# A searched issue order in which the two halves of 235 epilogue pairs stand as entries of their own

## The chip, the cores and the metric

The kernel runs on one core of a Trainium2 chip. The metric is the device time of one execution in microseconds (us). Its engines work side by side, each on its own list of instructions, in the order of that list: TensorE (PE; its weight loads are PEld), VectorE (DVE), ScalarE (ACT), GpSimd (POOL), and SyncE (SP), which only issues DMAs here. An instruction that needs another engine's result waits on a semaphore, and whatever stands behind it on its engine waits with it.

## The reference

The first part is an attention in which a query sees only the keys of its own cluster (4 batches, 8 heads, 768 positions, head size 64, 16 clusters); the second is a dense layer, a rational function and another dense layer over the 3072 tokens that come out.

```python
q_assign = np.argmax(einsum('bhsd,hcd->bhsc', q_n, c_n), axis=-1)   # k_assign likewise
mask = q_assign[:, :, :, None] == k_assign[:, :, None, :]
scores = np.where(mask, scale * (q @ k.transpose(0, 1, 3, 2)), -1e9)
attn = exp(scores - scores.max(-1)); attn = attn / (attn.sum(-1) + 1e-9)
x = (attn @ v).transpose(0, 2, 1, 3).reshape(3072, 512)
h = x @ w_in                                                        # 512 -> 2048
P = a[0] + a[1] * h + a[2] * h**2 + a[3] * h**3
Q = 1.0 + abs(b[0]) * abs(h) + abs(b[1]) * h**2
out = (P / (Q + 1e-6)) @ w_out                                      # 2048 -> 512
```

## The kernel before

The work is staged by batch (4), in a batch by pairs of heads (4) and by blocks of 256 queries (3). For each pair of heads, q and k are loaded, scaled and split into two fp16 halves, the clusters are found (`ptl` on PE at L1058, then on DVE `mx` L1072, `df` L1073, `df` L1076, `mxi` L1081, `oh` L1082), and the one-hot rows are written beside the operands (`tk` L1100) and turned by DMA. Batch 0 takes another path than the rest: scores with the keys on the partitions (`z` L1330), then `px` at L1349, sums at L1355, a reciprocal that is spread over the partitions on PE (`px` L1383), and the scaled result on DVE (`rw` L1392). Batches 1 to 3 compute `s` (L1162, a PSUM tile for 128 queries of one head), take the maximum on DVE (L1191), the exponential on ACT, the reciprocal of the sum (`su` L1210), and split the weights into `ah` (a high part on ACT, the rest on DVE at L1222, which is the last reader of the PSUM tile of `s`); a DMA turns them and PE multiplies them with v (`px` L1242). `vm`, `vt` and `vb` (L779 to L786) are the maximum of |v| of a batch.

The dense part of a block runs between these. It has 8 chunks of the 2048 columns, each in halves of 128 x 512 elements. `ph` (L1450) is x @ w_in in PSUM; 96 such halves are in the program. Each `ph` is read four times: by ACT (`u`, absolute value, and `t`, scale and offset) and by DVE (`t` at L1467 and `t` at L1468). POOL then computes the quadratic of Q (`s` at L1515, `s` at L1516; in a share of the halves ACT does the first), ACT a logarithm and an exponential of it, POOL the Newton factor (L1538), POOL or DVE the last step of P and its product with 1/Q (`t` at L1544 and L1545, or L1551), DVE the corrected quotient (L1556), then it is split into two fp16 halves (ACT L1560, POOL L1564) for the second matmul `po` (L1575). ACT instructions are all shown with L395, the line of a helper.

No instruction is issued while the program is written out: each becomes an entry of a list (`Plan.op`), numbered as it arises, and `Plan.emit` runs the entries in the order of the list `ORDER`, 4184 numbers that a search outside the program found. This one order decides the order on every engine, of the DMAs on SP, and which buffer of a ring a tile gets. An entry can hold several instructions; these then stand one behind the other on their engine, whatever the order says. Three such entries matter here:

```python
def poly(t=t, h=h, ph=ph, col=col):
    stt(out=t[h].ap, in0=ph.ap, scalar=col("rho")(), in1=t[h].ap, op0=ALU.mult, op1=ALU.mult)
    stt(out=t[h].ap, in0=t[h].ap, scalar=col("a1")(), in1=ph.ap, op0=ALU.add, op1=ALU.mult)
```

`poly` is on DVE (L1467 and L1468, 96 times), `square` on POOL (L1515 and L1516, 96 times), `times` on POOL (L1544 and L1545, 43 times).

Of the kernel before, what the change touches and what calls it, by code (L numbers as in the profile page):

```python
# [15 lines left out]
ALU = mybir.AluOpType  # L16
# [230 lines left out]
def clustered_attention_moe_kernel(  # L247
# [12 lines left out]
    nc = tc.nc  # L260
# [1149 lines left out]
    def moe(b, tb, vt):  # L1410
# [7 lines left out]
        for ci in range(NWC):  # L1418
# [5 lines left out]
            def col(name, ci=ci):  # L1424
                return lambda: gk.ap[:, COLS.index(name), ci : ci + 1]
# [240 lines left out]
```

## Time and profile before

| | before |
|---|---|
| runs, us | 930.46, 930.63, 931.91 (median 930.63) |
| the profiled execution's span, us | 930.4 |
| busy: PE | 863.5 us (93%) |
| busy: DVE, ACT, POOL | 835.6 (90%), 811.2 (87%), 729.3 us (78%) |
| chain that ended last | PE 54%, DVE 19%, ACT 9%, POOL 6%, issue 6%, DMA 5% |

The span of the profiled execution is 0.2 us under the median of the runs. Busy time is the time in which an engine has an instruction under way, summed over the whole span. The chain that ended last is followed back from the last instruction, at each step to what released it. No engine is idle for long, so what counts is in which stage an engine waits, and for whom; the page's 40 slices show PE below 90% in the first five of them, about 116 us.

### The profile page before, as it was taken

The page shows a single profiled execution, that of the slowest core. Times are in us where ns is not written, and L with a number is a line of the kernel's source. Part 1 is how long each engine was busy: PE and PEld are TensorE (multiplying, and loading weights), DVE is VectorE, ACT ScalarE, POOL GpSimd, SP SyncE. Part 2 cuts the span into 40 slices and gives each one's busy share as a digit, 9 for nine tenths or more (in the row PEclk, how much of TensorE's full clock was granted, in tenths as well). Part 3 has the DMA queues.
Part 4 walks back from the last instruction along what each step waited for, and adds up shares of the span by engine and source line. Part 5 has one row for each costly group of instructions (what it writes and reads, how often), then busy time and mean ns, then how long its engine had stood idle before and what let it go on. Part 6 is the DMA issues. An engine that isn't in the chain of part 4 may idle for free.

```text
span 930.4 us, 20764 instructions
## 1 busy us (share of the span) xinstructions
PE 863.5 (93%) x7705; PEld 581.1 (62%) x7705; DVE 835.6 (90%) x1503; ACT 811.2 (87%) x1558; POOL 729.3 (78%) x771
## 2 busy tenths in 40 slices
PE   1679998988899999999989999999999999999997
PEld 1357665656566666666666766666666675777663
DVE  6789999769989999999999999999999998899986
ACT  5577697989999999999999999999999998886774
POOL 2546789988999999999989988988989996464342
PEclk9989999989999999999999999999999999999999
DMA  7995765796977899998799879896987587501000
GB/s 200 232 249 130 190 193 148 177 230 138 188 133 154 164 161 203 155 167 163 155 162 180 164 135 169 178 188 110 208 150 150 92 165 130 121 2 33 8 24 23
DMA packets 360853, 137.70 MB, mean 148 GB/s; under 512 B 335665, under 2 KB 352049, under 8 KB 360753
## 3 DMA queue, kind: packets, MB, share of 16 engines
q1 hardware_dynamic: 360752, 136.39, 72.0%
q8 instruction: 60, 0.98, 0.4%
q14 instruction: 41, 0.33, 0.1%
HBM read 41.98 MB, written 6.29 MB: 52 GB/s over the span
## 4 chain that ended last, share of the span: by engine, by line
PE 54%; DVE 19%; ACT 9%; POOL 6%; issue 6%; DMA 5%; SPq 1%; ACTq 0%; DVEq 0%; POOLq 0%
PE ph L1450 18%; PE po L1575 18%; PE s L1162 7%; PE px L1242 5%; DVE ah L1222 3%; DVE s L1191 3%; DMA rvm<-in_v_dram 2%; PE s L1286 2%; DVE t L1467 1%; DVE t L1556 1%; ACT s L395 1%; PE px L1349 1%; DVE t L1468 1%; DVE top L1295 1%; PE z L1330 1%
## 5 line engine op out<-in xcount | busy, mean ns | idle before, releaser
L1450 PE MATMUL ph<-x,win 128*128 128x256 f16 x2304 | 273.1, 273 | 6.3 <-DVE t L1468 4.7
L1450 PEld LDWEIGHTS <-win 128*128 128x128 f16 x2304 | 223.2, 98 | 55.3 <-DVE t L1468 8.6
L1575 PE MATMUL po<-wout,s 128*128 128x512 f16 x1008 | 239.3, 379 | 0.7 <-POOL s L1564 0.7
L1191 DVE TENSOR_SCALAR_CACHE_REDUCE s<-s,cc 128x768 f32<-128x768 f32 x144 | 145.9, 1017 | 15.4 <-PE s L1162 14.8
L1575 PEld LDWEIGHTS <-s 128*128 128x128 f16 x1008 | 96.4, 98 | 101.2 <-issue 2.2
L1222 DVE SCALAR_TENSOR_TENSOR ah<-s,su,ah 128x768 f16<-128x768 f32 x144 | 144.9, 1011 | 5.6 <-ACT ah L395 5.3
L395 ACT ACTIVATE ah<-s,su 128x768 f16<-128x768 f32 x144 | 129.0, 901 | 7.8 <-DVE su L1210 7.2
L395 ACT ACTIVATE s<-s,nm 128x768 f32<-128x768 f32 x144 | 126.1, 876 | 7.3 <-DVE s L1191 4.9
L1162 PE MATMUL s<-sk,sq 128*128 128x384 f16 x576 | 117.8, 329 | 8.9 <-DVE ah L1222 7.9
L1516 POOL TENSOR_TENSOR s<-s,u 128x512 f32<-128x512 f32 x84 | 114.4, 1362 | 7.0
L1538 POOL TENSOR_TENSOR s<-s,u 128x512 f32<-128x512 f32 x72 | 99.1, 1378 | 7.0 <-ACT u L395 6.7
L1515 POOL TENSOR_SCALAR s<-u,g 128x512 f32<-128x512 f32 x84 | 69.6, 829 | 36.4 <-ACT u L395 33.6
L1564 POOL TENSOR_TENSOR s<-t,s 128x512 f16<-128x512 f32 x72 | 88.1, 1226 | 8.8 <-ACT s L1560 6.8
L1162 PEld LDWEIGHTS <-sq 128*128 128x128 f16 x576 | 52.2, 98 | 53.7 <-DVE ah L1222 17.9
L1556 DVE SCALAR_TENSOR_TENSOR t<-s,t 128x512 f32<-128x512 f32 x84 | 81.8, 973 | 0.8 <-POOL s L1538 0.5
L1242 PE MATMUL px<-at,vhi 128*64 128x256 f16 x864 | 75.2, 276 | 0.0
L395 ACT ACTIVATE u<-ph,gk 128x512 f32<-128x512 f32 x84 | 57.8, 688 | 9.3 <-PE ph L1450 8.7
L1468 DVE SCALAR_TENSOR_TENSOR t<-t,gk,ph 128x512 f32<-128x512 f32 x84 | 62.8, 748 | 3.0
L395 ACT ACTIVATE t<-ph,gk 128x512 f32<-128x512 f32 x84 | 65.4, 780 | 0.0
L1467 DVE SCALAR_TENSOR_TENSOR t<-ph,gk,t 128x512 f32<-128x512 f32 x84 | 62.1, 739 | 1.1 <-ACT t L395 1.0
L1545 POOL TENSOR_TENSOR t<-t,u 128x512 f32<-128x512 f32 x43 | 57.6, 1340 | 3.6
L1242 PE MATMUL px<-at,vlo 128*64 128x256 f16 x432 | 59.7, 273 | 0.0
(232 smaller groups left out, 1751.3 us busy)
## 6 DMA issues: line engine op xcount, KB each, us to landing
rwi<-in_moe_w_in_dram SPq DMA_DIRECT2D x16, 512.0 KB, 4.1
rwo<-in_moe_w_out_dram SPq DMA_DIRECT2D x16, 512.0 KB, 4.4
rk<-in_k_dram SPq DMA_DIRECT2D x32, 192.0 KB, 3.4
rq<-in_q_dram SPq DMA_DIRECT2D x32, 192.0 KB, 3.7
rvm<-in_v_dram SPq DMA_DIRECT2D x16, 384.0 KB, 3.8
rv<-in_v_dram SPq DMA_DIRECT2D x16, 384.0 KB, 4.1
out_dram<-ob SPq DMA_DIRECT2D x24, 256.0 KB, 2.9
sk<-sk SPq DMA_DIRECT2D x12, 192.0 KB, 3.4
```

What stands on the lines that cost most here:

```text
L395: lambda: nc.scalar.activation(out=out(), in_=in_(), func=func, **{a: (x() if callable(x) else x) for a, x in kw.items()}),
L1162: nc.tensor.matmul(sc.ap[:, i, :SH], lhsT=st["q" + x].ap[:, j, t, :], rhs=st["k" + x].ap[:, j, ks, :].rearrange("p t c -> p (t c)"), start ...
L1191: lambda nm=nm, view=view: ts(out=view(), in0=view(), scalar1=cc.ap[:, 0:1], scalar2=None, op0=ALU.mult, op1=ALU.min, accum_out=nm.ap),
L1222: lambda part=part, view=view, su=su: stt(out=part(1), in0=view(), scalar=su.ap, in1=part(0), op0=ALU.mult, op1=ALU.subtract),
L1242: nc.tensor.matmul(px.ap[j * D : (j + 1) * D, :], lhsT=vv.ap[:, j, kt, :], rhs=at[j].ap[:, p_, kt].rearrange("p t c -> p (t c)"), start=(i ...
L1450: nc.tensor.matmul(ph.ap[:, fi * TW : (fi + 1) * TW], lhsT=win[:, wpart, c, f * P : (f + 1) * P], rhs=xs[c].ap[:, xpart], start=(i == 0), ...
L1468: stt(out=t[h].ap, in0=t[h].ap, scalar=col("a1")(), in1=ph.ap, op0=ALU.add, op1=ALU.mult)
L1516: nc.gpsimd.tensor_tensor(out=sv(), in0=sv(), in1=uv(), op=ALU.mult)
L1538: lambda uv=uv, sv=sv: nc.gpsimd.tensor_tensor(out=sv(), in0=sv(), in1=uv(), op=ALU.mult),
L1556: lambda tv=tv, sv=sv: stt(out=tv(), in0=sv(), scalar=2.0, in1=tv(), op0=ALU.subtract, op1=ALU.mult),
L1564: lambda tv=tv, g16=g16, e=(nc.vector if kshare("gld", b, i_) else nc.gpsimd): e.tensor_tensor(out=g16(1), in0=tv(), in1=g16(0), op=ALU.su ...
L1575: nc.tensor.matmul(po[ti].ap, lhsT=g16(gg)[:, c0 : c0 + P], rhs=wout[:, wpart, f, :], start=(i == 0 and f == 0), stop=(i == 2 and f == NF ...
```

## The change

`ORDER` is replaced by another list, and the two instructions of each `poly`, `square` and `times` become two entries, so that the list has 4419 numbers. The operations, their operands, the tiles and the numbers of instructions on each engine stay as they are. The first half of `times` no longer names `u` as something it reads.

```diff
 ORDER = [int(i) for i in """
-3 376 377 28 375 374 4 5 6 40 7 8 0 9 379 381 382 10 29 383 32 30 388 31 391 380 33 34 392 44 384 41 490 42
...
-                def poly(t=t, h=h, ph=ph, col=col):
-                    stt(out=t[h].ap, in0=ph.ap, scalar=col("rho")(), in1=t[h].ap, op0=ALU.mult, op1=ALU.mult)
-                    stt(out=t[h].ap, in0=t[h].ap, scalar=col("a1")(), in1=ph.ap, op0=ALU.add, op1=ALU.mult)
-                dve(1523, poly, [ph, gk], [t[h]], u_ + h + kb("phr", b), [t_t], n=2)
+                dve(
+                    739,
+                    lambda t=t, h=h, ph=ph, col=col: stt(
+                        out=t[h].ap, in0=ph.ap, scalar=col("rho")(), in1=t[h].ap, op0=ALU.mult, op1=ALU.mult
+                    ),
+                    [ph, gk], [t[h]], u_ + h + kb("phr", b), [t_t],
+                )
+                dve(
+                    748,
+                    lambda t=t, h=h, ph=ph, col=col: stt(
+                        out=t[h].ap, in0=t[h].ap, scalar=col("a1")(), in1=ph.ap, op0=ALU.add, op1=ALU.mult
+                    ),
+                    [ph, gk], [t[h]], u_ + h + kb("phr", b), [t_t],
+                )
...
-                    def square(uv=uv, sv=sv):
-                        nc.gpsimd.tensor_scalar(out=sv(), in0=uv(), scalar1=g1c(BT), scalar2=1.0, op0=ALU.add, op1=ALU.mult)
-                        nc.gpsimd.tensor_tensor(out=sv(), in0=sv(), in1=uv(), op=ALU.mult)
-                    op("POOL", (2330, 3930)[k], square, [*us, g1], ss, uu + kb("sq", b), [s_t, u_t])
...
+                        [gk], tss, uu + kb("mul", b) - 0.2, [t_t],
```

`square` and `times` are parted in the same way. In the new order 43 of the 96 `poly` pairs have other DVE instructions between their halves (1 to 8), 38 of the 96 `square` pairs and 35 of the 43 `times` pairs other POOL instructions. Before, ACT's two reads of every `ph` stand ahead of DVE's two. Now that is so for 67 of them (for 17 more, ACT reads in the other order, t first), and in 12 ACT's absolute value comes behind a DVE read of the same tile: behind the first in 5, behind both in 7. The engines read one PSUM tile in turn, so each such place is a wait of one engine on another: 28 such waits of ACT on DVE and 13 of DVE on ACT, where there were 9 and none. On PE, 558 of 813 groups of matmuls stand at another place, by 1.8 places in the mean and 36 at most. Lines of the changed kernel are 11 higher up to `ph` (L1450 is L1461) and 34 higher from L1551 on (L1551 is L1585).

The first place is on DVE in the first 30 us, where the clusters of the first pair of heads are found (`mx0_0`, `df0_0`, `mxi0_0`, `oh0_0`, `tk20_0`) between the splitting of weights (`wwo`, L544 and L551). Before:

```order
L1010 SCALAR_TENSOR_TENSOR tk10_1_217<-rk0_1_178,ksc0_1_234,tk10_1_217 128x12x64
L544 TENSOR_SCALAR wwo0_0_304<-mwo0_0_300 128x512
L1072 TENSOR_REDUCE mx0_0_323<-ptl0_0_247 128x24
L551 SCALAR_TENSOR_TENSOR wwo0_0_304<-rwo0_0_226,wwo0_0_304 128x512
L1073 TENSOR_TENSOR df0_0_329<-ptl0_0_247,mx0_0_323 128x384
L1076 TENSOR_TENSOR df0_0_329<-df0_0_329,w16_74 128x384
L1081 TENSOR_REDUCE mxi0_0_340<-df0_0_329 128x24
L1082 TENSOR_TENSOR oh0_0_344<-df0_0_329,mxi0_0_340 128x384
L1100 TENSOR_SCALAR tk20_0_185<-oh0_0_344 128x12x48
```

The same stretch of DVE in the changed kernel:

```order
L1021 SCALAR_TENSOR_TENSOR tk10_1_218<-rk0_1_180,ksc0_1_227,tk10_1_218 128x12x64
L1083 TENSOR_REDUCE mx0_0_299<-ptl0_0_250 128x24
L1084 TENSOR_TENSOR df0_0_301<-ptl0_0_250,mx0_0_299 128x384
L555 TENSOR_SCALAR wwo0_0_305<-mwo0_0_303 128x512
L1087 TENSOR_TENSOR df0_0_301<-df0_0_301,w16_74 128x384
L562 SCALAR_TENSOR_TENSOR wwo0_0_305<-rwo0_0_231,wwo0_0_305 128x512
L1092 TENSOR_REDUCE mxi0_0_316<-df0_0_301 128x24
L1093 TENSOR_TENSOR oh0_0_318<-df0_0_301,mxi0_0_316 128x384
L1111 TENSOR_SCALAR tk20_0_205<-oh0_0_318 128x12x48
```

`mx` and the first `df`, the two readers of `ptl`, moved ahead of the first split of `wwo`, which waits for ACT's `mwo`.

The second place is on PE at the end of batch 0, where the maximum of |v| of batch 1 is turned (`vt1`) and the scores of its first block begin (`s1_0_0_1`, `s1_0_0_0`). Before:

```order
L1330 MATMUL z0_3_2_1_0_2682<-sq20_3_1769,sk20_3_1779 128x256
L1383 MATMUL px0_3_1_2594<-rw0_3_1_2669,pick_90 128x128 x2
L781 MATMUL vt1_2711<-ident_65,vm11_2705 1x128
L1162 LDWEIGHTS sq11_0_2202
L1162 MATMUL s1_0_0_1_2714<-sk11_0_2196,sq11_0_2202 128x384
L1162 LDWEIGHTS sq21_0_2565
L1162 MATMUL s1_0_0_1_2714<-sk21_0_2560,sq21_0_2565 128x384
```

The changed kernel on PE there, beginning with the third and fourth matmul of `s1_0_0_1` (the two ahead of them read alike, and ahead of those stand the last ones of `z0_3_2_1_1`):

```order
L1173 LDWEIGHTS sq11_0_2329
L1173 MATMUL s1_0_0_1_2683<-sk11_0_2277,sq11_0_2329 128x384
L1173 LDWEIGHTS sq21_0_2563
L1173 MATMUL s1_0_0_1_2683<-sk21_0_2561,sq21_0_2563 128x384
L792 MATMUL vt1_2688<-ident_65,vm11_2650 1x128
L1173 LDWEIGHTS sq11_0_2329
L1173 MATMUL s1_0_0_0_2690<-sk11_0_2277,sq11_0_2329 128x384
```

The four matmuls of `s1_0_0_1` moved ahead of `vt1`, and the spreading of `px0_3_1` (L1383) behind both score tiles.

The third place is on DVE in the middle of batch 2, ahead of its first `ah` of the second pair of heads; `mx2_2` and `df2_2` belong to the clusters of the third pair. Before:

```order
L1551 SCALAR_TENSOR_TENSOR t1_1_0_0_6622<-t1_1_0_0_6622,gk1_2792,u1_1_0_0_6594 128x512
L1210 RECIPROCAL su2_1_0_1_6878<-su2_1_0_1_6878 128x1
L1072 TENSOR_REDUCE mx2_2_6897<-ptl2_2_6829 128x24
L1222 SCALAR_TENSOR_TENSOR ah2_1_0_0_6887<-s2_1_0_0_6755,su2_1_0_0_6784,ah2_1_0_0_6887 128x768
L1222 SCALAR_TENSOR_TENSOR ah2_1_0_1_6899<-s2_1_0_1_6803,su2_1_0_1_6878,ah2_1_0_1_6899 128x768
L1073 TENSOR_TENSOR df2_2_6914<-ptl2_2_6829,mx2_2_6897 128x384
L1191 TENSOR_SCALAR s2_1_1_0_6906,nm2_1_1_0_6923<-s2_1_1_0_6906,cc2_1_5640 128x2x384
```

The same stretch of the changed kernel, also on DVE:

```order
L1233 SCALAR_TENSOR_TENSOR ah2_1_0_0_6789<-s2_1_0_0_6742,su2_1_0_0_6773,ah2_1_0_0_6789 128x768
L1083 TENSOR_REDUCE mx2_2_6872<-ptl2_2_6823 128x24
L1233 SCALAR_TENSOR_TENSOR ah2_1_0_1_6876<-s2_1_0_1_6765,su2_1_0_1_6780,ah2_1_0_1_6876 128x768
L1084 TENSOR_TENSOR df2_2_6879<-ptl2_2_6823,mx2_2_6872 128x384
L1479 SCALAR_TENSOR_TENSOR t1_1_1_0_6884<-ph1_1_1_0_6792,gk1_3490,t1_1_1_0_6884 128x512
L1202 TENSOR_SCALAR s2_1_1_0_6912,nm2_1_1_0_6917<-s2_1_1_0_6912,cc2_1_5506 128x2x384
L1486 SCALAR_TENSOR_TENSOR t1_1_1_0_6884<-t1_1_1_0_6884,gk1_3490,ph1_1_1_0_6792 128x512
```

`mx2_2` moved behind `ah2_1_0_0`, and a maximum of `s` (L1202) now stands between the halves of a `poly`. On PE, 12 matmuls of `po` instead of 6 stand between `ptl2_2` and `s2_1_1_0`.

## Rows read from the trace of the kernel before

**Rows 1.** The page: busy time of each engine.

```profile
PE 863.5 (93%) x7705; PEld 581.1 (62%) x7705; DVE 835.6 (90%) x1503; ACT 811.2 (87%) x1558; POOL 729.3 (78%) x771
```

**Rows 2.** Busy time of each engine by stretch of the span.

```profile
core 0: us, PE busy (x) PEld busy (x) DVE busy (x) ACT busy (x) POOL busy (x), PEclk, DMA share, GB/s
0.00:100.00 100.00, 66.36 (x670) 45.07 (x671) 78.30 (x178) 64.26 (x114) 52.67 (x73) 0.97 0.82 202
100.00:200.00 100.00, 89.69 (x1087) 63.62 (x1088) 85.50 (x159) 81.98 (x157) 86.14 (x104) 0.97 0.72 184
200.00:300.00 100.00, 93.23 (x844) 63.94 (x841) 88.12 (x163) 96.25 (x196) 90.76 (x97) 0.99 0.75 158
300.00:775.00 475.00, 464.10 (x4033) 310.00 (x4031) 449.35 (x818) 456.89 (x903) 431.94 (x445) 1.00 0.87 161
775.00:925.00 150.00, 149.05 (x1074) 98.20 (x1071) 134.31 (x189) 110.59 (x191) 67.76 (x56) 1.00 0.20 42
```

**Rows 3.** Waits, 300 to 775 us: total, times, longest (us).

```profile
PE s L1162 <- DVE ah L1222: 6.7, 12, 2.1
...
PE ph L1450 <- DVE t L1468: 2.3, 5, 0.7
```

**Rows 4.** Timeline of PE and DVE, first 30 us: start, duration, wait.

```profile
22.70 0.79 PE L1058 MATMUL ptl<-cen,sk 128*128 128x16 f16 x24
...
25.53 0.43 DVE L544 TENSOR_SCALAR wwo<-mwo 128x512 int32<-128x512 int32 x1 [1.85 <-ACT mwo L395]
25.88 0.55 DVE L1072 TENSOR_REDUCE mx<-ptl 128x24 f32<-128x384 f32 x1
26.34 0.68 DVE L551 SCALAR_TENSOR_TENSOR wwo<-rwo,wwo 128x512 int32<-128x512 int32 x1
...
27.53 0.36 DVE L1076 TENSOR_TENSOR df<-df,w 128x384 bf16<-128x384 bf16 x1
27.92 0.55 DVE L1081 TENSOR_REDUCE mxi<-df 128x24 bf16<-128x384 bf16 x1
28.51 0.56 DVE L1082 TENSOR_TENSOR oh<-df,mxi 128x384 f16<-128x384 bf16 x1
29.10 0.31 DVE L1100 TENSOR_SCALAR tk<-oh 128x576 f16<-128x576 f16 x1
```

**Rows 5.** Timeline of PE around 194 us.

```profile
193.90 0.27 PE L781 MATMUL vt<-ident,vm 128*1 128x128 f32 x1 [1.48 <-DVE rw L1392]
194.01 2.58 PE L1162 MATMUL s<-sk,sq 128*128 128x384 f16 x8
...
197.46 4.57 PE L1349 MATMUL px<-at,rv 128*64 128x256 f32 x24 [0.35 <-ACT vp_ln L395]
```

**Rows 6.** The same 24 matmuls of an earlier block, timeline of PE.

```profile
166.94 2.81 PE L1349 MATMUL px<-at,rv 128*64 128x256 f32 x24
```

**Rows 7.** Busy time by engine, 194 to 201 us; columns as in Rows 2.

```profile
194.00:201.00 7.00, 6.65 (x29) 3.41 (x29) 4.43 (x11) 5.91 (x14) 6.54 (x10) 0.52 1.03 258
```

**Rows 8.** Timeline of PE and DVE around 475 us.

```profile
472.00 1.46 PE L1575 MATMUL po<-wout,s 128*128 128x512 f16 x6
475.60 1.75 PE L1162 MATMUL s<-sk,sq 128*128 128x384 f16 x8 [2.14 <-DVE ah L1222]
477.19 1.03 PE L1575 MATMUL po<-wout,s 128*128 128x512 f16 x4
...
474.09 0.53 DVE L1072 TENSOR_REDUCE mx<-ptl 128x24 f32<-128x384 f32 x1
474.54 1.93 DVE L1222 SCALAR_TENSOR_TENSOR ah<-s,su,ah 128x768 f16<-128x768 f32 x2
```

**Rows 9.** Groups by line: busy us, mean ns, idle time before them.

```profile
L1468 DVE SCALAR_TENSOR_TENSOR t<-t,gk,ph 128x512 f32<-128x512 f32 x84 | 62.8, 748 | 3.0
...
L1556 DVE SCALAR_TENSOR_TENSOR t<-s,t 128x512 f32<-128x512 f32 x84 | 81.8, 973 | 0.8 <-POOL s L1538 0.5
```

**Rows 10.** A single instruction of L1556, timeline of DVE.

```profile
306.41 0.68 DVE L1556 SCALAR_TENSOR_TENSOR t<-s,t 128x512 f32<-128x512 f32 x1
```

More of the change, by code (lines that the diff above doesn't have):

```diff
@@ L1512, in moe @@
                 else:
-                    def square(uv=uv, sv=sv):
-                        nc.gpsimd.tensor_scalar(out=sv(), in0=uv(), scalar1=g1c(BT), scalar2=1.0, op0=ALU.add, op1=ALU.mult)
-                        nc.gpsimd.tensor_tensor(out=sv(), in0=sv(), in1=uv(), op=ALU.mult)
-                    op("POOL", (2330, 3930)[k], square, [*us, g1], ss, uu + kb("sq", b), [s_t, u_t])
+                    op(
+                        "POOL", 829,
+                        lambda uv=uv, sv=sv: nc.gpsimd.tensor_scalar(
+                            out=sv(), in0=uv(), scalar1=g1c(BT), scalar2=1.0, op0=ALU.add, op1=ALU.mult
+                        ),
+                        [*us, g1], ss, uu + kb("sq", b), [s_t, u_t],
+                    )
+                    op(
+                        "POOL", 1362,
+                        lambda uv=uv, sv=sv: nc.gpsimd.tensor_tensor(out=sv(), in0=sv(), in1=uv(), op=ALU.mult),
+                        [*us, g1], ss, uu + kb("sq", b), [s_t, u_t],
+                    )
                 acq = kshare("acq", b, i_)
@@ L1541, in moe @@
                 if mulp or swap:
-                    def times(tv=tv, uv=uv, col=col):
-                        nc.gpsimd.tensor_scalar(out=tv(), in0=tv(), scalar1=col("a0")(), scalar2=1.0, op0=ALU.add, op1=ALU.mult)
-                        nc.gpsimd.tensor_tensor(out=tv(), in0=tv(), in1=uv(), op=ALU.mult)
-                    op("POOL", (2183, 3840)[k], times, [*us, gk], tss, uu + kb("mul", b), [t_t, u_t])
+                    op(
+                        "POOL", 847,
+                        lambda tv=tv, col=col: nc.gpsimd.tensor_scalar(
+                            out=tv(), in0=tv(), scalar1=col("a0")(), scalar2=1.0, op0=ALU.add, op1=ALU.mult
+                        ),
+                        [gk], tss, uu + kb("mul", b) - 0.2, [t_t],
+                    )
+                    op(
+                        "POOL", 1340,
+                        lambda tv=tv, uv=uv: nc.gpsimd.tensor_tensor(out=tv(), in0=tv(), in1=uv(), op=ALU.mult),
+                        [*us, gk], tss, uu + kb("mul", b), [t_t, u_t],
+                    )
                 else:
```

372 rows, old and new, of the table ORDER are left out of this document.

## The prediction

> **What bounds the kernel now.** I read the busy times first, and the reader is to see there that no engine is free: PE is busy for 93% of the span, DVE 90%, ACT 87%, POOL 78% [rows 1]. Such a share is a mean over stages with different limits, so the second view is the busy time by stretch [rows 2]. PE is idle for 100 − 66.36 = 33.6 us in the first 100 us, 10.3 in the second, 6.8 in the third, 10.9 in the 475 us after it, and 0.95 in the 150 us from 775 on. An order of work can win only what an engine spends waiting, so at the end there is nothing, and in the long steady stretch at most 10.9 us of 475. In that stretch DVE (449.35 of 475) and ACT (456.89) are nearly as full as PE: DVE has 25.7 us of slack, ACT 18.1. An engine that is let off one wait there soon meets the next.
>
> Third, the chain of waits of that stretch [rows 3]: what PE waits for longest is a score tile that DVE has not yet read for the last time (12 waits, 6.7 us, 2.1 at most); the waits that `poly` itself makes (5, 2.3 us) are few. Last, the timeline at the largest single waits, three of which the new order touches.
>
> **The change part by part.** No instruction is added or removed, so nothing has a price of its own; all of it is waits taken away, moved or made. I went through the order of both kernels on every engine, and counted, at each PE group, the DVE, ACT and POOL work that must be done ahead of it. All along the program this moves by 1 to 5 us in either direction, so the stages keep their shape, and no stage changes its bound. What changes are places.
>
> *The head, at 25 us.* DVE waits 1.85 us for ACT's `mwo` with `mx` queued behind, though `ptl` was done at 22.70 + 0.79 = 23.49 [rows 4]. In the new order `mx` and `df` run in that wait. Behind it stand, as now, 0.43 (L544), 0.36 (L1076), 0.68 (L551), 0.55 (L1081) and 0.56 us (L1082): 25.53 + 2.58 = 28.1 for the start of `tk`, where it was 29.10. That is 1.0 us. Below it is nothing, since DMAs fill 0.82 of this stretch [rows 2] and the operand may wait in their queue anyway; above it is the whole wait, 1.85. I take 1.0, because what stands between is counted row by row.
>
> *The end of batch 0, at 194 us.* PE waits 1.48 us ahead of `vt` [rows 5], and the scores behind it wait for nothing that the profile shows. In the new order four of their matmuls, half of the 2.58 us, run first: 1.29 us, which all but fills the wait, and what `vt` waited for is then there. I take 1.5; between 0 (if the operands of the scores come late too) and 1.5.
>
> *The middle of batch 2, at 475 us.* PE waits 2.14 us for `ah`, which stood behind `mx`; `mx` takes 474.54 − 474.09 = 0.45 us of DVE [rows 8], and now stands behind it. On PE, 6 more matmuls of `po` stand ahead of the waiting scores. Six took 1.46 and four 1.03, so one takes 0.215 and six more cover 1.29. Together 1.75 of 2.14, between 0 (they are only moved from a place where they covered something else) and 2.1.
>
> *The parted pairs.* Between the halves of a `poly` DVE stands still for 3.0/84 = 36 ns [rows 9]. Where another instruction now stands between, that is filled: 43 x 36 ns = 1.5 us of DVE time. It reaches the end only where DVE is what PE waits for, so I take half, 0.8, between 0 and 1.5. On POOL the same costs and gives nothing: with 78% [rows 1] it is ahead of those that read it.
>
> *The reads of `ph`.* In 12 places ACT's absolute value now stands behind a DVE read of the same PSUM tile and waits for it. The price is between nothing and one `poly` instruction each, 62.8/84 = 0.75 us [rows 9]: 12 x 0.75 = 9.0 us of ACT time. I take nothing. At the first such tile of the batches 1 to 3 (`ph1_1_0_0`) ACT has eight other instructions ahead of the absolute value, one of which itself waits for a DVE instruction that stands behind both reads, so the tile is free by then; an order that puts the reads late on ACT puts them behind work that takes longer than the DVE read. The Trainium skill speaks against the change here: "PSUM — Partial Sum Buffer", section "PSUM bank collisions raise a hardware error", says that accesses of two engines to one bank must be guarded by a semaphore, reads against reads of ACT and DVE included, so that these reads can't overlap and must be paid somewhere. The trace has ACT and DVE read `ph` one after the other, but no price for an exposed wait of ACT there; by the page the sum would lose up to the bound just given.
>
> *All other places.* Of 17 waits of PE over 0.3 us between 100 and 200 us, 14 now have more PE work ahead of them in proportion to the other engines' work that they need, 1.1 us in the mean; from 200 us on as many lose as gain. Of the 10.3 us there [rows 2], 1.5 are counted above; of the other 8.8 I take a quarter, 2.2, because most of such a lead is again lost at the next wait. Between 0 and 8.8.
>
> The sum: 1.0 + 1.5 + 1.75 + 0.8 + 0 + 2.2 = 7.25. The steady stretch gives half of its 1.75 + 0.8 back, 1.3, since ACT has only 18.1 − 10.9 = 7.2 us more slack than PE there. That leaves 6.0: from the profiled execution's 930.4, 924.4. This execution stands 0.2 us under the median of the runs, so the forecast is 924.5 us.
>
> **The rivals.**
>
> *Slower, by the reads of `ph`.* The 12 absolute values of ACT wait for DVE, ACT passes `u` on late to POOL, and the second matmul comes late. For it: ACT is full to 96% between 300 and 775 us. Against it: the place looked at above, and that most of these reads were put behind other ACT work. Its price is 9.0 us; with the gains of 6 it comes out at 930.4 − 6.0 + 9.0 = 933.4. It decides once more than about 6.0/0.75 = 8 of the 12 waits stand open for their whole length. Chance 0.15.
>
> *Slower, by DVE and POOL getting in each other's way.* L1556 takes 973 ns in the mean [rows 9] and 0.68 us when it is left alone [rows 10]: 84 x 0.29 = 25 us of DVE time go there already, and as much again may lie in like instructions. A parted order may bring more of them beside POOL's. A third more of the 25, 8 us, would give 930.4 + 8 − 6 = 932.4. The Trainium skill has the rule in "SBUF — State Buffer", section "Who interferes with whom": a DVE instruction with two inputs in SBUF contends with a GpSimd instruction that reads SBUF, and which was issued first decides who is blocked. By that rule, with which the two durations of L1556 agree, only the alignment of the two engines counts, and no count of instructions tells its sign. Chance 0.08.
>
> *No difference.* The places are better one by one, but DVE and ACT set the pace, and each gain is lost at the next wait: about 930. For it: the slack of DVE and ACT in [rows 2]; that the amount of work needed ahead of each PE group hardly moves. Against it: the gains of the first 200 us lie where these engines wait as well. Chance 0.15.
>
> *A larger gain.* At 194 us the granted clock falls to 0.52, the 1.2 GHz level, until 201 [rows 7]; right ahead of it PE had stood still for 1.48 us. The 24 matmuls of L1349 took 4.57 us there [rows 5] against 2.81 elsewhere [rows 6], and eight of L1162 took 2.58 against 1.75 [rows 8]: 1.76 + 0.83 = 2.6 us. If the clock stays up with the wait filled, that comes on top; and if of the 8.8 us of other waits two thirds go, not a quarter, another 3.7: 924.4 − 6.3 = 918. Chance 0.24; the forecast has the remaining 0.38.
>
> **How the numbers follow.** About 0.2% (1.9 us) is what a measurement of this kernel can tell from no change. Faster by more than that are the forecast and the larger gain, 0.38 + 0.24 = 0.62; the same, 0.15; slower, 0.15 + 0.08 = 0.23. The two slower cases with their prices lie at 932.4 and 933.4; the waits on `ph` could cost more where they hold up POOL too, so the range ends at 935. Below, all bounds at once (1.85 + 1.5 + 2.1 + 1.5 + 8.8 = 15.75, with the clock's 2.6 and without what is given back: 912) are unlikely, and I end at 915. The forecast's own range is 920 to 928.
>
> **What the profile after would show.** In the first 30 us, `tk` at L1111 starts at about 28.1. At 192 to 194 us PE has no wait over 0.5 us ahead of `vt` (now L792). At about 470 us the wait of the scores (L1173) for `ah` (L1233) is under 0.5. PE's idle time in 100 to 200 us is 6 to 7 us where it was 10.3, and that of 300 to 775 about 9.5 where it was 10.9. ACT's instructions `u` that wait for DVE's `t` on `ph` should hardly appear in the chain of waits, and the mean of L1556 (now L1590) stays within 30 ns of 973. The prediction is wrong if ACT shows waits on L1479 or L1486 of several us, if that mean moves, or if the stretch from 200 to 775 us, which I have nearly even, changes by more than 3 us.

## The result, and the profile after

The changed kernel is slower: 942.66 us (median of 4 runs, 941.63 to 944.66) against 930.55 us for the kernel before (4 runs beside it), a ratio of 1.0132 with a 95% interval of [1.0108, 1.0157]. That is 12 us, outside the predicted range and on the other side of no change.

The page of the changed kernel: busy time of each engine, and the chain that ended last.

```profile
PE 863.8 (92%) x7705; PEld 586.7 (62%) x7705; DVE 822.4 (87%) x1503; ACT 816.9 (87%) x1558; POOL 708.9 (75%) x771
...
PE 41%; ACT 18%; DVE 13%; DMA 10%; POOL 10%; issue 5%; SPq 2%; ACTq 0%; DVEq 0%; POOLq 0%
```

PE is busy for as long as in [rows 1] (863.8 against 863.5 us); what was added is waiting. DVE and POOL are even busy for 13 and 20 us less. On the chain, DMA went from 5 to 10%, ACT from 9 to 18%.

Busy time by stretch, columns as in [rows 2]:

```profile
0.00:100.00 100.00, 67.15 (x682) 45.71 (x682) 80.01 (x181) 66.94 (x117) 57.42 (x75) 0.97 0.85 211
100.00:200.00 100.00, 90.14 (x1183) 65.33 (x1182) 78.99 (x158) 82.16 (x161) 78.63 (x97) 0.98 0.74 181
200.00:300.00 100.00, 91.87 (x742) 64.13 (x738) 87.18 (x165) 93.63 (x188) 90.22 (x98) 0.95 0.70 140
300.00:775.00 475.00, 453.91 (x3933) 305.16 (x3932) 438.59 (x795) 449.60 (x880) 406.48 (x428) 0.99 0.85 160
775.00:925.00 150.00, 150.00 (x1130) 101.67 (x1129) 132.72 (x201) 120.05 (x210) 74.19 (x74) 1.00 0.27 52
```

Against [rows 2], PE waits a little less in the first 200 us and twice as much between 300 and 775: 475 − 453.91 = 21.1 us where it was 10.9. For whom it waits, between 200 and 775 us (total, times, longest):

```profile
PE s L1173 <- DVE ah L1233: 10.1, 19, 2.0
PE px L1253 <- DMA at<-ah: 6.5, 4, 2.3
PE ptl L1069 <- DMA sq<-tq: 3.8, 1, 3.8
PE ph L1461 <- DVE qsc L972: 2.7, 1, 2.7
...
PE s L1173 <- DMA sk<-sk: 1.2, 1, 1.2
...
PE s L1173 <- DMA sq<-sq: 0.5, 1, 0.5
```

Four of these rows name a DMA, 12.0 us together; before, no wait of PE for a DMA stands in this view of the same stretch. All rows of the view added up: 16.5 us before, 28.1 after.

Where the time goes can be followed instruction by instruction, since both kernels hold the same ones: the end of each ACT instruction in the changed kernel less its end in the kernel before, and of these the median in stretches of 25 us. The changed kernel is ahead by 3.5 us at 175, by 2.8 at 225, level at 300, 2.1 behind at 400, 7.3 at 425, 5.7 at 475, 8.6 at 525, 9.9 at 600 and 10.9 at 775. So it wins 3 to 4 us in the first 200 us and loses some 14 behind them, in steps. (The two traces differ by 940.1 − 930.4 = 9.7 us and the medians by 12.1, since the profiled execution of the kernel before was one of its longer ones.) The largest step, at 419 us, on the timeline of PE and of SP (L1037 turns q and k; in neither trace does an issue of SP begin before the last thing that it waits for):

```profile
406.81 1.56 PE L1173 MATMUL s<-sk,sq 128*128 128x384 f16 x8
...
406.45 1.02 SPq L420 DMA_DIRECT2D rq<-in_q_dram  x2
407.52 0.47 SPq L420 DMA_DIRECT2D rk<-in_k_dram  x1
408.10 0.38 SPq L420 DMA_DIRECT2D rv<-in_v_dram  x1
408.58 1.30 SPq L1240 DMA_TRANSPOSE at<-ah  x1
409.97 4.12 SPq L1037 DMA_TRANSPOSE sk<-tk  x1
414.14 1.50 SPq L1037 DMA_TRANSPOSE sq<-tq  x1
...
414.66 0.82 PE L1173 MATMUL s<-sk,sq 128*128 128x384 f16 x4 [0.19 <-DVE ah L1233]
419.32 0.81 PE L1069 MATMUL ptl<-cen,sq 128*128 128x16 f16 x24 [3.84 <-DMA sq<-tq]
```

And the busy time ahead of and behind that wait:

```profile
408.00:419.00 11.00, 7.29 (x67) 4.51 (x64) 9.63 (x16) 10.60 (x21) 10.92 (x10) 0.99 1.17 213
419.00:425.50 6.50, 6.18 (x64) 3.54 (x65) 1.95 (x3) 1.30 (x3) 1.21 (x2) 0.50 0.94 202
```

The turn of k needs a tile that the scores of an earlier pair of heads have read, and these end at 408.4, so it waits for nothing more when its issue begins. That issue takes 4.12 us, the longest of the 212 turns in this trace (mean 1.8). The turn of q stands behind it and lands at 419.3, and `ptl` is already the next thing on PE. Directly ahead on SP stand four loads and a turn of weights. In the kernel before, PE has the same order at this place, but three of these loads stand behind the two turns and the fourth (v) at 478.6 us; its SP:

```profile
405.93 1.42 SPq L1026 DMA_TRANSPOSE sk<-tk  x1
407.39 1.95 SPq L1026 DMA_TRANSPOSE sq<-tq  x1
...
413.21 0.59 SPq L409 DMA_DIRECT2D rk<-in_k_dram  x1
...
417.20 1.46 SPq L409 DMA_DIRECT2D rq<-in_q_dram  x2
```

There the turn of q lands at 413.3 and PE does not wait for it. In the traces of all 20 kernels of this case the issue of this turn takes 2.3 to 4.1 us in the ten in which the four loads stand within 6 us ahead of it, and 1.4 to 2.2 us in the ten in which they do not. So the long issue goes with the loads, but no run moved them alone, and what they cost at the end is not shown. While PE waits in the changed kernel, the other engines finish what they have (ACT is busy for 10.60 of 11 us); then PE works at a granted clock of 0.50, the 1.2 GHz level, for 6.5 us, and DVE, ACT and POOL are all but empty.

### The profile page after: what moved, and what is told of

Same layout as the page of the kernel before. It is cut to its first block, busy times and chain, and to the rows that moved or that the text cites. A ratio compares the mean times of both kernels' runs of the same rounds, so it can differ in the third digit from the quotient of the medians.

```text
span 940.1 us, 20759 instructions
## 1 busy us (share of the span) xinstructions
PE 863.8 (92%) x7705; PEld 586.7 (62%) x7705; DVE 822.4 (87%) x1503; ACT 816.9 (87%) x1558; POOL 708.9 (75%) x771
## 4 chain that ended last, share of the span: by engine, by line
PE 41%; ACT 18%; DVE 13%; DMA 10%; POOL 10%; issue 5%; SPq 2%; ACTq 0%; DVEq 0%; POOLq 0%
PE po L1609 14%; PE ph L1461 13%; ACT s L406 5%; PE s L1173 4%; PE px L1253 4%; DMA sq<-tq 3%; ACT u L406 3%; ACT ah L406 3%; DMA at<-ah 2%; DVE ah L1233 2%; DVE s L1202 2%; POOL s L1543 1%; ACT t L406 1%; POOL s L1565 1%; DVE top L1306 1%
## 5 line engine op out<-in xcount | busy, mean ns | idle before, releaser
L1461 PE MATMUL ph<-x,win 128*128 128x256 f16 x2304 | 270.5, 274 | 3.4 <-DVE qsc L972 2.7
L1461 PEld LDWEIGHTS <-win 128*128 128x128 f16 x2304 | 226.0, 98 | 47.0 <-DVE t L1486 4.7
L1202 DVE TENSOR_SCALAR_CACHE_REDUCE s<-s,cc 128x768 f32<-128x768 f32 x144 | 145.5, 1016 | 16.7 <-PE s L1173 15.9
L1543 POOL TENSOR_TENSOR s<-s,u 128x512 f32<-128x512 f32 x84 | 111.4, 1328 | 3.9
L1565 POOL TENSOR_TENSOR s<-s,u 128x512 f32<-128x512 f32 x72 | 96.3, 1339 | 10.0 <-ACT u L406 8.3
L1590 DVE SCALAR_TENSOR_TENSOR t<-s,t 128x512 f32<-128x512 f32 x84 | 79.5, 948 | 2.3 <-POOL s L1565 0.6
L1579 POOL TENSOR_TENSOR t<-t,u 128x512 f32<-128x512 f32 x43 | 60.6, 1408 | 6.2 <-ACT u L406 3.5
L1486 DVE SCALAR_TENSOR_TENSOR t<-t,gk,ph 128x512 f32<-128x512 f32 x84 | 62.4, 742 | 1.7
L1253 PE MATMUL px<-at,vlo 128*64 128x256 f16 x432 | 61.8, 276 | 0.0
```

The costliest lines, as they stand in the source:

```text
L1202: lambda nm=nm, view=view: ts(out=view(), in0=view(), scalar1=cc.ap[:, 0:1], scalar2=None, op0=ALU.mult, op1=ALU.min, accum_out=nm.ap),
L1253: nc.tensor.matmul(px.ap[j * D : (j + 1) * D, :], lhsT=vv.ap[:, j, kt, :], rhs=at[j].ap[:, p_, kt].rearrange("p t c -> p (t c)"), start=(i ...
L1461: nc.tensor.matmul(ph.ap[:, fi * TW : (fi + 1) * TW], lhsT=win[:, wpart, c, f * P : (f + 1) * P], rhs=xs[c].ap[:, xpart], start=(i == 0), ...
L1543: lambda uv=uv, sv=sv: nc.gpsimd.tensor_tensor(out=sv(), in0=sv(), in1=uv(), op=ALU.mult),
L1565: lambda uv=uv, sv=sv: nc.gpsimd.tensor_tensor(out=sv(), in0=sv(), in1=uv(), op=ALU.mult),
L1590: lambda tv=tv, sv=sv: stt(out=tv(), in0=sv(), scalar=2.0, in1=tv(), op0=ALU.subtract, op1=ALU.mult),
```

## The experiments

All are the changed kernel's code with other entries in `ORDER`. "before" in the diffs is the order of the kernel before with the halves of each pair side by side, which makes that kernel again; "changed" is the new order. Ratios are to the kernel before, run beside each.

**The parting of the pairs.** First the changed order with all 235 pairs rejoined (one of the pairs on DVE, from the third place shown ahead):

```diff
 DVE L1479 t1_1_1_0
+DVE L1486 t1_1_1_0
 DVE L1202 s2_1_1_0
-DVE L1486 t1_1_1_0
```

> The changed kernel's order, with the two halves of all 235 parted pairs put side by side again (poly and square at the place of the first half, times at the place of the second); nothing else moves. Theory (the time is lost on SP's queue: PE waits for DMAs in the changed kernel, 15 us in waits over 0.5 us, where it waits for none before): the parting has little to do with it, and the time stays at 942 within 2 us. Rival (the parted pairs and the reads of ph that wait for each other cost the time): it falls to about 930.

959.02 us, ratio 1.0316 [1.0287, 1.0346]: 16 us slower than with the pairs parted (959.0 − 942.7). With its pairs rejoined in this way the changed order is slower still, so the parting is not what makes it slow. The mirror parts 42 poly pairs in the order before:

```diff
 DVE L1467
+DVE (the next instruction)
 DVE L1468
-DVE (the next instruction)
```

> The kernel before with 42 of the 43 poly pairs that the changed kernel parts on DVE parted in the same way: the second half stands behind the next DVE instruction (in 17 of them a reciprocal of 157 ns, the others 0.4 to 1.1 us). The orders of PE, ACT, POOL and SP stay exactly as they are. If parting by itself costs (ph, which the second half frees, comes free later, and what reads t waits): up to 42 x 0.6 = 25 us of delay, of which what PE waits for shows, 3 to 10 us slower. If it gains (36 ns each): 0.5 to 1.5 us faster. My theory, that the loss is in the order of the stretches and not in the parting: within 3 us of the kernel before.

936.01 us, 1.0083 [1.0053, 1.0112]. In an order that was made for whole pairs the parting costs 7 us. The waits of PE from 200 to 930 us show where a part of it goes:

```profile
PE s L1172 <- DVE ah L1232: 10.9, 18, 2.2
PE ph L1460 <- DVE t L1485: 7.3, 10, 1.6
```

Before these two were 7.9 (15) and 4.7 us (8): PE gets the PSUM tiles later. Whether the parting costs or gains depends on the order around it.

**SP's order, whole.** The engines' order of one kernel with the DMAs' order of the other:

```diff
-{"PE": changed, "DVE": changed, "ACT": changed, "POOL": changed, "SP": changed}
+{"PE": changed, "DVE": changed, "ACT": changed, "POOL": changed, "SP": before}
```

> PE, DVE, ACT and POOL in the order of the changed kernel (two ACT instructions differ), the 391 DMAs of SP in the order of the kernel before, save 64 that the new order of the other engines forces to other places, by 36 at most. Theory (SP's order): the waits of PE for DMAs go, and the time falls to 926 to 932. Rival (the pairs): it stays at 940 to 943. A second rival, that the two orders only fit together: above 945.

> The mirror: PE, DVE, ACT and POOL in the order of the kernel before (18 instructions displaced, by 12 at most), the DMAs of SP in the order of the changed kernel. Theory (SP's order alone is bad): PE waits for DMAs as in the changed kernel, 938 to 946. Rival (the pairs): 930 to 932, as before.

1021.74 us (1.0992 [1.0973, 1.1011]) and 1027.15 us (1.1048 [1.1021, 1.1075]): both 90 us and more behind. The five lists of an order fit each other; the test was too coarse to tell anything of SP's order. In the first, PE waits in this view (200 to 930 us) for turns of weights that stand on SP behind others. The four longest of these waits are 7.6 to 14.9 us, and the turns that end them are issued 18 to 23 us after all that they themselves wait for is there:

```profile
PE px L1252 <- DMA at<-ah: 46.7, 7, 14.9
```

**The waits for DMAs, one by one.** In the changed kernel 22 of 114 turned or copied tiles that PE first reads after 200 us land less than 0.5 us ahead of that read; before it was 2 of 116. And a turn of attention weights (`at` from `ah`, 144 of them) is issued 5.39 us in the mean after its source is ready, before 3.09, while its issue (1.7 us) and landing (2.7 us) take the same. So I moved single DMAs ahead of loads (first diff), or PE's reader behind other matmuls (second):

```diff
 SP at1_0_2_0<-ah1_0_5_0
-SP rvm3_1<-in_v_dram
 SP at1_0_2_1<-ah1_0_5_1
-SP rvm3_2<-in_v_dram
 SP at1_0_2_1<-ah1_0_4_1
+SP rvm3_1<-in_v_dram
+SP rvm3_2<-in_v_dram
```

> The changed order with six edits on SP alone: five DMAs that turn operands of PE, and one copy, stand ahead of loads of later data (or of another turn) where they stood behind them; 24 of 391 DMAs change places, and 20 DVE and ACT instructions swap with a neighbour. In the changed kernel PE waits at these places for the landing, 1.96 (at 265 us), 1.17 (310), 0.68 (450), 2.28 (532) and 1.62 us (672), 7.7 in all. Theory (the changed order spends the slack between a DMA's landing and PE's use of the tile, 22 of 114 tiles under 0.5 us against 2 of 116 before): 6 to 8 us less, 935 to 937. Rival (those waits only take the place of others that would come behind): 940 to 943.

```diff
-PE px2_1_2
 PE s2_2_1_0
 PE po
 PE po
+PE px2_1_2
```

> The changed order with the DMAs as they are; on PE the first consumers of six late tiles stand 2 to 4 groups later, behind matmuls that do not need them. The waits there are 11.5 us in all (3.84 at 419 us with a stretch at the 1.2 GHz level behind it, 2.28, 1.96, 1.62, 1.17, 0.68). Theory (slack): 8 to 12 us less, 930 to 935. Rival (they are replaced by waits of others, since the consumers' results come later): 940 to 945.

944.37 us (1.0169 [1.0140, 1.0199]) and 946.53 us (1.0186 [1.0153, 1.0219]): nothing won. In the first, a new wait stands at the place of the wait of 1.96 us (timeline of PE):

```profile
265.56 0.37 PE L957 MATMUL kt<-ident,sumk 128*1 128x128 f32 x1 [3.43 <-ACT tk L405]
```

In the second, the timeline of PE at the places where it waited 1.96 and 2.28 us for a DMA:

```profile
266.08 0.82 PE L1172 MATMUL s<-sk,sq 128*128 128x384 f16 x4 [1.94 <-DVE ah L1232]
...
536.42 0.82 PE L1172 MATMUL s<-sk,sq 128*128 128x384 f16 x4 [2.05 <-DVE ah L1232]
```

The reader is to compare the lengths: a wait as long as before stands there, now at the scores and for DVE. Next all 144 turns by the time at which they were ready, with the other engines untouched; and two edits in the order before:

```diff
-SP: changed
+SP: sorted(changed, key=ready)
```

> PE, DVE, ACT and POOL exactly in the order of the changed kernel; on SP the 144 turns of attention weights (at from ah) stand by the time at which their source was ready and a buffer free in the changed kernel's trace, so that 58 DMAs come earlier, by 10 places at most, and the loads that they pass later by 3 at most. In the changed kernel a turn is issued 5.39 us after its source is ready in the mean, before 3.09; issue and landing take the same in both. Theory (turns stand on SP behind turns whose source is ready later, so that PE finds its tiles late): 930 to 937. Rival (SP only shows the delay; PE then waits for DVE and ACT at the same places): 940 to 945.

> The mirror in the kernel before: PE, DVE, ACT and POOL exactly in its order, and on SP, in 22 of 72 tiles, the turn whose source is ready first moved behind the tile's other turn, as the changed kernel has it in these 22 tiles (26 in all, before 12). 89 DMAs change places, most by one. Theory (turns that wait behind later ones): 5 to 12 us slower than the kernel before, 935 to 942. Rival (the turns have slack enough): within 2 us of the kernel before.

> The kernel before with its turns by readiness on SP, 41 DMAs earlier by 7 places at most, the other engines untouched. If turns that wait on SP cost time in the kernel before too (12 tiles inverted, 3.09 us in the mean): 1 to 4 us under it. If its turns have slack enough (2 of 116 tiles land under 0.5 us ahead of their use): within 1 us of it.

943.64 us (1.0147 [1.0124, 1.0171]), 931.06 (1.0018 [1.0004, 1.0031]) and 929.76 (0.9998 [0.9984, 1.0013]). My theory, that the time lost is the time for which turns stand on SP, fell: with the turns of weights issued 2.27 us after they are ready, less than in the kernel before, the changed order is no faster, and the order before loses only 1.4 us when turns stand behind later ones. In the first of the three, two waits at `ptl` (timeline of PE) had grown to hold most of the loss:

```profile
419.92 0.81 PE L1068 MATMUL ptl<-cen,sq 128*128 128x16 f16 x24 [4.84 <-DMA sq<-tq]
...
682.14 0.77 PE L1068 MATMUL ptl<-cen,sq 128*128 128x16 f16 x24 [4.60 <-DMA sq<-tq]
```

Two further runs went at these, on SP alone and on SP and PE:

```diff
 SP sk12_1<-tk12_1
+SP sq12_1<-tq12_1
 SP at1_3_2_1<-ah1_3_4_1
-SP sq12_1<-tq12_1
```

> Of the run above only the edit on SP: the turn of q right behind that of k at 413 and at 672 us, two DMAs moved and six places changed; PE, DVE, ACT and POOL exactly in the order of the changed kernel. By the timeline the two turns then land 3 and 5 us earlier, so that of 943.6 some 7 go if PE's wait for them is the loss: 935 to 938. Rival (other waits take their place): 941 to 945.

> The run with the turns by readiness (943.6 us), in whose trace nearly all that it loses on the kernel before is lost in three steps, each at a PE instruction ptl that waits for a turned q or k: 4.84 us at 420, 1.37 at 583 and 4.60 at 682 us; a px waits 1.80 at 530. Here the turn of q stands right behind that of k on SP at 413 and 672 us, and on PE the ptl at 420 and at 583 us and the px at 530 us stand 2 to 3 groups later (14 PE places, 16 of DVE, ACT and POOL by a neighbour). Theory (these waits are the loss): 930 to 935. Rival (PE has nothing else ready at these places, so another wait stands there): 940 to 945.

942.79 us (1.0147 [1.0127, 1.0168]) and 947.26 (1.0194 [1.0162, 1.0226]). In the first, the wait at 682 us is gone and that at 420 still 3.46 us. In the second, PE at the same place (timeline):

```profile
422.63 2.50 PE L1608 MATMUL po<-wout,s 128*128 128x512 f16 x6 [2.32 <-ACT ob L405]
```

The matmuls put ahead of `ptl` to cover its wait were not ready either. The waits of PE from 200 to 775 us, each view's rows added up by what ended them (us):

| run | DMA | DVE | ACT, POOL, issue | all |
|---|---|---|---|---|
| before | 0 | 15.2 | 1.3 | 16.5 |
| changed | 12.0 | 14.1 | 2.0 | 28.1 |
| turns ahead of loads | 9.5 | 13.3 | 7.0 | 29.8 |
| readers later on PE | 2.4 | 26.3 | 3.0 | 31.7 |
| turns by readiness | 14.5 | 12.4 | 1.5 | 28.4 |
| the same, q behind k | 10.9 | 12.7 | 3.4 | 27.0 |
| the same, `ptl` and a `px` later too | 1.3 | 19.9 | 6.9 | 28.1 |

Whatever is taken away, 27 to 32 us stay. But the two runs that took most of the waits for DMAs away did it by moving PE's readers; in the three that moved DMAs and left PE's order as it is, 9.5 to 14.5 us of these waits stay, and in every changed order of this table the four loads stand ahead of the two turns at 410 us. So the table shows that moving PE's readers only gives the wait another name; that late landings do not cause a part of the loss is not shown.

**By stretches.** An order can be cut where nearly the same entries stand ahead of the cut in both:

```diff
-ORDER = before
+ORDER = changed[:746] + [i for i in before if i not in changed[:746]]
```

The first run was cut at 900 entries, where 12 stand on the wrong side; the others at better places.

> The first 900 entries of the changed order (about 200 us of the span), then all that is left in the order of the kernel before. At 200 us the changed kernel is 3 to 4 us ahead of the kernel before. Theory (the loss lies behind 200 us, and the lead of the head holds): 926 to 928. Rival (the lead is lost at the next wait whatever comes behind): 930 to 931.

> The first 746 entries of the changed order (to about 167 us), then what is left in the order of the kernel before; 5 entries stand on the wrong side of this seam, where the run before had one with 12 and lost 5 to 6 us there. Theory (the head is better, the rest worse, and a clean seam costs nothing): 3 us under the kernel before, 926 to 928. Rival (the rest only fits its own head): 930 to 936.

> The mirror: the first 746 entries in the order of the kernel before, the rest in the changed one. Theory (the loss lies behind 167 us): the changed kernel's time and the 3 us of its head on top, 944 to 947. Rival (the changed rest only suffers from its own head, or the loss lies in the head): 931 to 940.

> The kernel before with the entries from about 167 to 405 us in the changed order. There the changed kernel goes from 4 us ahead to 2 behind. Theory (the loss belongs to the order of each stretch, and the stretches add up): 5 to 7 us slower than the kernel before, 934 to 936. Rival (the changed order loses there only behind its own head): 928 to 931.

> The kernel before with the entries of one stretch, from about 405 to 490 us, in the changed order (4 entries stand on the wrong side of its first seam, 4 of the second). In this stretch the changed kernel loses 4 to 5 us on the kernel before, nearly all at one wait of PE for a turned q at 419 us (3.84 us, and a stretch at the 1.2 GHz level behind it). Theory (the loss lies in the order of that stretch): 933 to 936. Rival (it comes from what is behind or ahead, or from the state in which the changed order arrives there): 928 to 931.

> The kernel before up to about 490 us, then the changed order. From there the changed kernel loses 3 to 4 us in its trace (6.5 behind at 490, 10 at the end). Theory (stretches add up): 932 to 934. Rival (it loses there only by what it brings along): 928 to 931.

> The mirror: the changed kernel with the entries from about 405 to 490 us in the order of the kernel before. Theory (the loss lies in the order of that stretch): 4 to 6 us under the changed kernel, 936 to 939. Rival (the loss only moves to the next place): 941 to 944.

| changed order in | us | ratio |
|---|---|---|
| to 200 us (12 entries astray) | 936.16 | 1.0065 [1.0049, 1.0081] |
| to 167 us | 932.61 | 1.0034 [1.0013, 1.0055] |
| 167 to 405 us | 935.16 | 1.0063 [1.0038, 1.0088] |
| 405 to 490 us | 937.06 | 1.0075 [1.0050, 1.0100] |
| 490 us to the end | 932.96 | 1.0039 [1.0023, 1.0055] |
| all behind 167 us | 943.12 | 1.0155 [1.0123, 1.0187] |
| all but 405 to 490 us | 939.55 | 1.0095 [1.0065, 1.0125] |

Each run with one stretch exchanged is slower, and none gains, not even the head, though there the changed kernel's trace is 3 us ahead. The four stretches that make up the whole add to 2.1%, more than the 1.32% of the change. A rival that these runs can't exclude is the seam itself: the cut with 12 entries astray cost 3.6 us more than that with 5 (936.16 − 932.61), as much as a whole stretch, so what a stretch costs without its seams is not known. With 405 to 490 us put back into the order before, the changed kernel is 3 us faster, but the two intervals overlap. In the stretch from 405 to 490 us the loss is again a chain of waits; its largest (timeline of PE) stands at the second seam:

```profile
493.46 1.38 PE L1172 MATMUL s<-sk,sq 128*128 128x384 f16 x4 [3.39 <-DVE ah L1232]
```

## Why the prediction was wrong

**What bounds the kernel** was read rightly: no engine is free, and an order can only win what an engine waits. But I put the profiled execution 0.2 us under the median; in every run made since, of either kernel, the time is 1.7 to 2.2 us above the span, so this execution stood 1.5 to 2 us above its median. That moves the base of the sum, not its sign. (The 40 slices, too, were misread ahead: PE is below 90% in the first three, the seventh and the ninth to eleventh, not in the first five. The sum does not use them.)

**The places** came out one right, one at its lower bound, and one better by luck. In the head, and on PE at 194 and at 475 us:

```profile
19.74 0.79 PE L1069 MATMUL ptl<-cen,sk 128*128 128x16 f16 x24
...
24.50 1.33 DVE L1093 TENSOR_TENSOR oh<-df,mxi 128x384 f16<-128x384 bf16 x1
25.86 0.31 DVE L1111 TENSOR_SCALAR tk<-oh 128x576 f16<-128x576 f16 x1
...
190.89 0.66 PE L1173 MATMUL s<-sk,sq 128*128 128x384 f16 x3 [2.58 <-DMA sq<-sq]
...
481.81 1.46 PE L1173 MATMUL s<-sk,sq 128*128 128x384 f16 x8
```

`tk` starts at 25.86 (forecast 28.1, before 29.10 [rows 4]): a gain of 3.2, not 1.0. But `ptl` itself ends 3.0 us earlier, at 20.53 where it was 23.49, by what stands ahead of it; from there to `tk` it is 5.3 us where it was 5.6. The step that I had forecast gave 0.3 us: `mx` and `df` run without the wait, and `oh` took 1.33 us where it was 0.56. In the head run above none of the lead reaches the end. At 194 us PE came earlier and waited longer, for the copy of the second half of q: the operand that I had named as the case for nothing. At 475 us the wait of 2.14 us [rows 8] is gone, as forecast, and the lag falls from 7.3 to 5.7 us there.

**The reads of `ph`**, taken at nothing, cost next to nothing. The only wait of ACT for a poly instruction in its list of waits:

```profile
ACT u L406 <- DVE t L1486: 1.6, 1, 1.6
```

The Trainium skill's rule ("PSUM — Partial Sum Buffer", section "PSUM bank collisions raise a hardware error"), that reads of two engines must be guarded against each other, has a price here, 1.6 us against the bound of 9.0. The rival built on it was not what happened.

**DVE and POOL** got in each other's way less, not more. The groups that answer to [rows 9] (mean ns is the last number ahead of the second bar):

```profile
L1486 DVE SCALAR_TENSOR_TENSOR t<-t,gk,ph 128x512 f32<-128x512 f32 x84 | 62.4, 742 | 1.7
...
L1590 DVE SCALAR_TENSOR_TENSOR t<-s,t 128x512 f32<-128x512 f32 x84 | 79.5, 948 | 2.3 <-POOL s L1565 0.6 <-POOL t L1579 0.6
```

L1590 went from 973 to 948 ns, and DVE's whole busy time fell by 13 us, without any gain at the end: here a shorter busy time of an engine that waits on others was worth nothing. The idle time ahead of L1486 fell from 3.0 to 1.7 us, as the step on the pairs had it, but the pairs' price in the two orders, 16 us for and 7 against, has nothing to do with those 36 ns.

**The step that failed** is "all other places", and ahead of it the sentence that DVE, ACT and POOL work needed ahead of each PE group moves by 1 to 5 us and the stages keep their shape. I took shifts of 1 to 5 us for nothing, and the steps in which the loss comes are of that size (that they come from these shifts is not shown). The term was 2.2 us won. Between 100 and 200 us I counted 14 better places of 17, and PE's idle time there fell from 10.3 to 9.9 us, by 0.4, where the sum had 2.2 for these places and 1.5 for that at 194 us; from 200 us on "as many lose as gain" stood for 14 us lost, and PE's waits between 200 and 775 us rose from 16.5 to 28.1 us. A change of over 3 us there was a sign of being wrong that I had named. The count also left out SP: it weighed the work of three engines and not the queue of the turns nor the time to their landing, where the new waits first show. At 419 us that is the order of four loads and two turns. And the sum priced each place by itself, where in the runs a wait taken from one place came back at the next.

**What stays open.** The loss comes in steps along the whole program behind 225 us, no single stretch holds it, and each of the four stretches costs when it is exchanged alone, its seams included; that is shown. What sets the pace in them is not. At 419 us the four loads ahead of the two turns are the nearest rival, and the run that would decide is the changed order with these loads alone behind the turns; no run did it, for this place or for all.

## What to carry to other kernels

Where all engines are near full and the buffers between them few, an order is worth what its slack is worth: a search that prices waits between engines must price the queue of the DMAs and their landing too, and be judged on the chip, since here gains at single places did not add up. Before mending a wait, add up all waits of that engine and look at the sum after the edit: if the releaser changes and the sum stays, the edit has not reached the cause. To find out which part of a new order is bad, cut both orders where nearly the same entries stand ahead and run the parts, and reckon with what the seams cost; exchanging SP's whole list told nothing here. And look, at the largest new wait, at what stands ahead in the queue that it waits for, in both kernels.

## What the runs showed of the hardware

The turn of a tile costs twice: its issue holds SP for 1.7 us, and it lands 2.7 us after that (means of 144 in either kernel). Two turns directly behind four loads and a third turn were issued in 4.12 and 1.50 us, and the second landed 9.3 us after the first was begun (409.97 to 419.3); without the loads ahead, in the kernel before, 1.42 and 1.95 us and 7.3 us (405.93 to 413.3). And a single wait of PE of 3.84 us was followed by 6.5 us at a granted clock of 0.50, in which the other three engines were nearly empty: from 408 to 425.5 us PE was idle for 4.0 us, each of the others for 5.4 to 5.9.
